# A list scheduler's ranking with slack, a shorter landing margin, and x rows loaded as nine and eight, in the training step of a speech RNN-T joint

## The chip, the cores and the metric

One core of one Trainium2 chip runs the whole program. The metric is device time in microseconds (us), the median of several runs of one execution each. The core has five engines that work side by side: PE (TensorE, matmuls), ACT (ScalarE), DVE (VectorE), POOL (GpSimd) and SP (SyncE, which here only issues DMAs). They are tied together by semaphores; each engine takes its own instructions strictly in the order in which the program lists them.

## The reference

Forward pass of a small convolutional front end and a joint network, and the gradients of all of its inputs:

```python
def _fwd_reference(x, w1, w2, g, w_f, w_g, w_o):
    B, T, D = x.shape                       # 2, 16000, 256
    h = sum over i of einsum("btc,cd->btd", xp[:, i:i+T], w1[i])     # K = 3 taps, zero padded
    h = gelu(h)[:, ::2]                     # 8000 positions
    f = sum over i of einsum("btc,cd->btd", hp[:, i:i+T1], w2[i])
    f = gelu(f)[:, ::2]                     # 4000 positions
    fe = einsum("btd,de->bte", f, w_f)
    ge = einsum("bud,de->bue", g, w_g)      # g: 2 x 8 x 256
    j = tanh(fe[:, :, None, :] + ge[:, None, :, :])
    return einsum("btud,dv->btuv", j, w_o)  # 2 x 4000 x 8 x 256

out, vjp = jax.vjp(_fwd_reference, x, w1, w2, g, w_f, w_g, w_o)
return (out, *vjp(grad_out))                # grad_out: 2 x 4000 x 8 x 256
```

Everything in HBM is bf16. The output `out` and the given `grad_out` are the large arrays (33 MB each); x and its gradient have 16 MB each.

## The kernel before

**Tiling.** The 4000 positions of `f` of each batch are cut into chunks: batch 0 has one of 256, seven of 512 and one of 160, batch 1 seven of 512, one of 256 and one of 160; 18 chunks in all. A chunk of W positions uses 4W rows of x. Chunks of 512 and 256 are called whole, those of 160 are not (160 is no multiple of 128).

**Stages of a chunk.**

- `load_xc` brings the rows of x in, transposed by the DMA (tile XC: channels on partitions).
- `stage_a` computes the first convolution for odd and even positions (XC times W1, tiles HT), the second (HT times W2, tile FT) and FE = FT times WF. `conv_gelu` follows each convolution's matmuls with ACT's square and gelu and with DVE's work on the gelu's derivative (tiles g_sq, g_s, which end as G1o, G1e and G2). `to_rows` then turns FE by PE transposes (L656, PSUM tile psb) into a row form, FER.
- `stage_j` works on four pairs of the eight u. For each pair ACT computes tanh(FE + ge) in column form (JT, L788); DVE adds FER and GEB (JR, L801) and ACT takes its tanh (JR, L808) in row form. PE multiplies JR by grad_out (GWO, the gradient of w_o, kept in PSUM for the whole program); PE multiplies the transposed grad_out (GOT) by the transposed w_o (GOT,WT matmuls); a square of JT (JSQ, on ACT L845 or on DVE L847) and DVE's NGZ (L855) turn this into the gradient before the tanh, which ZS and in the end NGFE collect over u (L863); PE computes the output (WO,JT matmuls), which is cast to OUT_SB (ACT L423 or DVE L428) and stored.
- `stage_de` runs one chunk behind `stage_j`: NGFE times WFT gives GF (L943), GF times W2T gives GH (L971, L981), GH times W1T gives GX, the gradient of x (cast on ACT L425 or DVE L430, then stored). The weight gradients are matmuls of row forms (`wgrad`), each added by DVE to an accumulator in fp32 (ACC, L912). The gradient of w1 needs GH in rows (GHR, a DMA transpose) and rows of x (X, loaded by `load_x9` for whole chunks, by `load_x5` for the others).
- After the last chunk, DVE writes seven weight gradients as `w_out` tiles, and `store` and `gg_out` write the last ones.

The matmuls are all recorded by the helper `mm` (L412), the DMAs by `dma` (L438, L440).

**Rows of x.** Partition p of a whole chunk with nb blocks (4 for 512 positions, 2 for 256) holds nb consecutive positions. The gradient of w1 needs 5 rows of x for each position, 4 rows from one position to the next, thus 4 nb + 1 rows for each partition. `load_x9` brings 9 of these rows (9 x 256 values) in one load; a chunk of 512 has two such loads (h = 0 and 1), in the two buffers of class "x5", the second starting 8 rows after the first. `xrow` picks the row for block bl and tap f from them. All matmul groups of `wgrad` for w1 read both buffers.

**The order of the work.** Nothing is issued where it is written. The class `Flow` records each operation (`op`) with its engine or engines, a cost in ns from the small functions `c_pe`, `c_act`, `c_dve`, the buffers it reads and writes, and a position. `issue` then plays the whole program in a model, `run`: each engine e has a time T[e], and at each step the model looks at every operation whose inputs have been issued, takes for it the start s (the modelled end of its inputs plus a wake-up time WAKE, or the time at which a buffer of its class comes free), and picks, for each engine, the operation with the smallest pair (max(s, t), key). Among the engines the smallest pair wins. So an operation that can start now beats one that is more urgent but ready 10 ns later; among those that can all start at once the key decides. After a pass `backward` replaces the keys by the latest start times that this schedule allows; there are three such passes, the best order is kept and emitted. An operation with two engines in `eng` (casts by `evac`, JSQ, some shift copies) goes to whichever engine wins it, so the order also decides the engine.

A DMA is done in the model at

```python
o.done = ring[e] + 2000.0 + o.margin     # L241
```

where `ring` adds up the transfers' modelled durations (a transposing DMA `bytes / 256 * 1.25` ns) and `margin` is MARGIN = 6500 (L49) unless the call names another (FIRST = 500 for the first loads and weights, 2000 for grad_out of the first chunk). The margin is thus a time that the model leaves between the modelled arrival of data and the use of it; it makes SP issue the load earlier against the work, or the user wait in the model.

Buffers of a class are reused in turn: "go" (rows of grad_out) has 4, "got" (its transpose) 3, "x5" 2, PSUM "ps" 7.

Of the kernel before, what the change touches and what calls it, by code (L numbers as in the profile page):

```python
# [13 lines left out]
ACT = mybir.ActivationFunctionType  # L14
# [6 lines left out]
LOADQ, STOREQ = "SP", "SP"  # L21
# [22 lines left out]
class Flow:  # L44
# [1 line left out]


    WAKE = {"PE": 45.0, "ACT": 25.0, "DVE": 25.0, "POOL": 280.0, "SP": 60.0}
    MARGIN = 6500.0  # L49
    TAIL = {"PE": 180.0, "ACT": 130.0, "DVE": 95.0, "POOL": 40.0, "SP": 0.0}  # L50

    def __init__(self, ctx, tc):
# [9 lines left out]
    def buf(self, cls, shape, dtype, name):  # L62
        b = Buf(cls, shape, dtype, name)
        s = self.seq[cls]
        b.seq, s[0] = s[0], s[0] + 1
        return b
# [89 lines left out]
    def run(self, emit):  # L156
        T = {e: 0.0 for e in self.WAKE}
        avail = {e: [] for e in T}
        ring = {"SP": 0.0, "POOL": 0.0, "ACT": 0.0}
        lanes = {True: [], False: []}  # L160
        left, prog = len(self.ops), -1e12
        slots = {k: [[p, 0.0, []] for p, _, _ in v] for k, v in self.slots.items()}
        seq = {k: [v[0], 0, v[2]] for k, v in self.seq.items()}
        users, use = {}, {}
        for o in self.ops:
            o.left = 0
            for b in o.bufs:
                users[b] = users.get(b, 0) + 1
        for o in self.ops:
            for d in o.succ:  # L170
                d.left += 1
        num = 0

        def put(o):
            o.ready = max((d.done for d in o.deps), default=0.0)
            for e in o.eng:
                avail[e].append(o)

        for o in self.ops:
            if o.left == 0:  # L180
                put(o)
        while left:
            best = None
            for e, lst in avail.items():
                t, wake, cand = T[e], self.WAKE[e], None
                for o in lst:
                    if o.nb is not None and prog < o.nb:
                        continue
                    s = o.ready + wake
                    if o.work:  # L190
                        ln = lanes[e == "POOL"]
                        if len(ln) >= 8:
                            s = max(s, ln[-8] + wake)
                    for b in o.new:
                        st = seq[b.cls]
                        if not st[2] and st[1] != b.seq:
                            s = None
                            break
                        f = min((x[1] for x in slots[b.cls] if x[1] is not None), default=None)
                        if f is None:  # L200
                            s = None
                            break
                        s = max(s, f + wake)
                    if s is None:
                        continue
                    k = (max(s, t), o.key, o, e)
                    if cand is None or k < cand:
                        cand = k
                if cand is not None and (best is None or cand[0] < best[0]):
                    best = cand  # L210
            if best is None:
                prog = min((o.nb for lst in avail.values() for o in lst if o.nb is not None and o.nb > prog), default=None)
                assert prog is not None, "no operation can start"
                continue
            s, _, o, e = best
            if o.lead:
                prog = max(prog, o.pos)
            for x in o.eng:
                avail[x].remove(o)
            o.slotdeps = []  # L220
            for b in o.new:
                free = [i for i, x in enumerate(slots[b.cls]) if x[1] is not None]
                i = min(free, key=lambda i: (slots[b.cls][i][1], i))
                b.slot, slots[b.cls][i][1] = i, None
                if not seq[b.cls][2]:
                    o.slotdeps += slots[b.cls][i][2]
                slots[b.cls][i][2] = []
                seq[b.cls][1] += 1
                if emit:
                    b.t = slots[b.cls][i][0].tile(b.shape, b.dtype, name=b.name, tag=b.cls)  # L230
            T[e] = s + o.cost[o.eng.index(e)]
            if o.work:
                a = max(ring[e], T[e] - 400.0)
                if e == "POOL":
                    ring[e] = a + o.work
                    for q in ("SP", "ACT"):
                        if ring[q] > a:
                            ring[q] += o.work
                else:
                    ring[e] = max(a, ring["POOL"]) + o.work  # L240
                o.done = ring[e] + 2000.0 + o.margin  # L241
                lanes[e == "POOL"].append(o.done - o.margin)
            else:
                o.done = T[e] + self.TAIL[e]
            o.at, o.seqn = (e, s, T[e]), num
            num += 1
            if emit:
                o.inst = o.fn(e)
                for h in o.hold:
                    self.tc.add_manual_dep(o.inst.ins, h.inst.ins.name, mybir.DependencyInfo(  # L250
                        mybir.DependencyClass.Sync, mybir.DependencyReason.DATA), reason="order of the first loads")
            left -= 1
            for b in o.bufs:
                if b.cls is not None:
                    slots[b.cls][b.slot][2].append(o)
                users[b] -= 1
                if users[b] == 0 and b.cls is not None:
                    slots[b.cls][b.slot][1] = o.done
            for d in o.succ:
                d.left -= 1  # L260
                if d.left == 0:
                    put(d)
        return T["PE"] if not emit else T
# [15 lines left out]
def kernel(  # L279
# [20 lines left out]
    B, T, D = x.shape  # L300
# [7 lines left out]
    P = 128  # L308
# [125 lines left out]
    def dma(q, out, in_, r, w, bytes_, new=(), transpose=False, at=None, after=(), cost=None, hold=(), nb=None, margin=None):  # L434
        def go(e):
            eng_ = nc.sync if e == "SP" else nc.gpsimd if e == "POOL" else nc.scalar
            if transpose:
                return eng_.dma_start_transpose(out=out(), in_=in_())  # L438
            else:
                return eng_.dma_start(out=out(), in_=in_())  # L440
        c = 1260.0 if transpose else 400.0 if q == "SP" else cost or (750.0 if q == "POOL" else 100.0)
        return op(q, c, go, r=r, w=w, new=new, at=at, after=after, hold=hold, nb=nb, margin=margin,
                  work=bytes_ / 256 * 1.25 if transpose else bytes_ / 300.0)
# [75 lines left out]

    def load_x9(b, c0, nb, h, at, hold=()):  # L520

        X9 = buf("x5", [P, 9, D], BF16, "X9")
        src, new, r0 = x[b, 0:1, :], [X9], 0
        if c0 == 0 and h == 0:
            op("POOL", 150.0, lambda e: nc.gpsimd.memset(X9[0:1, 0:3, :], 0.0), w=[(X9, "a")], new=new, at=at)
            dma(LOADQ, lambda: X9[0:1, 3:9, :], lambda: x[b, 0:6, :].rearrange("(o f) d -> o f d", o=1),
                r=[], w=[(X9, "b")], bytes_=3072, at=at, cost=550.0)
            new, r0 = [], 1
        for k, (lo, hi) in enumerate(row_parts(r0, P)):
            dma(LOADQ, lambda lo=lo, hi=hi: X9[:].rearrange("p f d -> p (f d)")[lo:hi],  # L530
                lambda lo=lo, hi=hi: bass.AP(tensor=src.tensor, offset=src.offset + (4 * (c0 + nb * lo) - 3 + 8 * h) * D,
                                             ap=[[4 * nb * D, hi - lo], [1, 9 * D]]),
                r=[], w=[(X9, ("m", k))], bytes_=(hi - lo) * 4608, new=new, at=at, hold=hold, cost=550.0)
            new = []
        return X9

# [379 lines left out]
    def stage_de(g_, t0, dt):  # L916
        b, ci, c0, W = chunks[g_]
# [100 lines left out]
        hold_ = S["go"] if g_ < 2 else ()  # L1018
        if wh:
            X5 = [load_x9(b, c0, nb_of[g_], h, t0 + dt * 0.2, hold_) for h in range(nb_of[g_] // 2)]  # L1020
            xrow = lambda m, bl, f, d2: X5[bl // 2][:m, bl % 2 * 4 + f, d2 * P:(d2 + 1) * P]
        else:
            X5 = [load_x5(b, c0 + bl * P, min(P, Ws - bl * P), t0 + dt * 0.2, hold_) for bl, m in sblk]
            xrow = lambda m, bl, f, d2: X5[bl][:m, f, d2 * P:(d2 + 1) * P]
# [76 lines left out]
    def gg_out():  # L1101
# [43 lines left out]
       r=[(warm, 0)], w=[(warm, 1)])  # L1145
# [117 lines left out]
```

## Time and profile before

| what | before |
|---|---|
| runs (us) | 808.18, 805.31, 805.61, 808.00, 805.19 |
| median (us) | 805.61 |
| the profiled execution (us) | 808.18 |
| its span, first to last instruction (us) | 806.4 |
| PE's last matmul ends (us) | 799.1 |
| bytes moved by DMA, mean rate | 184.81 MB, 229 GB/s |
| POOL busy | 85.7 us, 11% |
| ACT tanh JT (L788), of the span | 183.1 us, 288 instructions |
| DVE NGZ (L855) | 151.8 us, 252 instructions |
| ACT tanh JR (L808) | 136.4 us, 128 instructions |
| landing of GOT (72 transposing DMAs), median | 6.6 us |
| landing of X (28 loads of 576 KB), median | 6.4 us |

The span is 1.8 us shorter than the time of the execution it comes from, and that execution was the slowest of the five. Busy time of one engine is the union of its instructions; in rows of a group, "busy" is that too, and the mean is the duration of one instruction, which for pipelined instructions is longer than their distance. In a line of the chain of waits, such as "PE GWO L412 <- ACT JR L808", the first part waits and the second is what ended last before it; the three figures are the microseconds in all, the number of waits and the longest. The granted clock is that of PE, 1.00 being full speed.

The stretches of the profile that the prediction uses are the start (0 to 20 us, loads and the first convolutions; 20 to 120, the first chunks), the long middle (120 to 795) and the end.

### The profile page before, as it was taken

The page shows a single profiled execution, that of the slowest core. Times are in us where ns is not written, and L with a number is a line of the kernel's source. Part 1 is how long each engine was busy: PE and PEld are TensorE (multiplying, and loading weights), DVE is VectorE, ACT ScalarE, POOL GpSimd, SP SyncE. Part 2 cuts the span into 40 slices and gives each one's busy share as a digit, 9 for nine tenths or more (in the row PEclk, how much of TensorE's full clock was granted, in tenths as well). Part 3 has the DMA queues.
Part 4 walks back from the last instruction along what each step waited for, and adds up shares of the span by engine and source line. Part 5 has one row for each costly group of instructions (what it writes and reads, how often), then busy time and mean ns, then how long its engine had stood idle before and what let it go on. Part 6 is the DMA issues. An engine that isn't in the chain of part 4 may idle for free.

```text
span 806.4 us, 16830 instructions
## 1 busy us (share of the span) xinstructions
PE 775.8 (96%) x6083; PEld 575.0 (71%) x6124; DVE 761.2 (94%) x1743; ACT 705.8 (88%) x1138; POOL 85.7 (11%) x256
## 2 busy tenths in 40 slices
PE   7889999999999999999999999999999999999996
PEld 6556668676776867777777667676776867778885
DVE  4989999999999999998989999999999999999894
ACT  5989999988898999997889999988898989997482
POOL 1001010100102001011010100000101001010121
PEclk9989999999999999999999999999999999999999
DMA  8999999999999999999999999999999999997995
GB/s 192 199 234 215 224 210 241 240 230 286 208 253 231 249 248 197 246 224 232 212 232 180 264 249 237 240 237 284 206 265 226 246 249 228 258 222 226 191 215 140
DMA packets 403360, 184.81 MB, mean 229 GB/s; under 512 B 326310, under 2 KB 394956, under 8 KB 403276
## 3 DMA queue, kind: packets, MB, share of 16 engines
q1 hardware_dynamic: 400764, 182.53, 102.5%
q10 hardware_dynamic: 2384, 1.18, 0.6%
q8 instruction: 48, 0.79, 0.4%
q14 instruction: 36, 0.29, 0.1%
q0 software_dynamic: 128, 0.03, 0.0%
HBM read 52.48 MB, written 50.34 MB: 128 GB/s over the span
## 4 chain that ended last, share of the span: by engine, by line
PE 46%; DVE 31%; ACT 17%; DMA 3%; issue 3%; SPq 1%; DVEq 0%; ACTq 0%
PE ps L412 39%; PE GWO L412 6%; DVE NGZ L855 6%; DVE ZS L863 5%; ACT JT L788 4%; ACT JSQ L845 3%; DVE g_s L603 3%; DVE JR L801 3%; ACT g_sq L599 2%; DVE ACC L912 2%; ACT JR L808 2%; ACT HT L601 2%; ACT OUT_SB L423 2%; DVE g_sq L614 2%; DMA X<-in_x_dram 1%
## 5 line engine op out<-in xcount | busy, mean ns | idle before, releaser
L788 ACT ACTIVATE JT<-FE,GE 128x512 bf16<-128x512 bf16 (+2 forms) x288 | 183.1, 676 | 7.9 <-PE ps L412 6.9
L412 PE MATMUL ps<-GOT,WT 128*128 128x512 bf16 (+3 forms) x640 | 152.5, 333 | 1.5 <-DVE NGZ L855 0.3
L412 PE MATMUL ps<-WO,JT 128*128 128x256 bf16 x1024 | 151.7, 272 | 2.3 <-DVE GH L981 1.7
L855 DVE SCALAR_TENSOR_TENSOR NGZ<-JSQ,ps 128x512 f32<-128x512 bf16 (+2 forms) x252 | 151.8, 607 | 0.0
L808 ACT ACTIVATE JR<-JR 128x1024 bf16<-128x1024 bf16 x128 | 136.4, 1071 | 9.1 <-DVE JR L801 9.0
L845 ACT ACTIVATE JSQ<-JT 128x1024 bf16<-128x1024 bf16 (+2 forms) x128 | 126.1, 985 | 15.6 <-DVE NGZ L855 14.7
L412 PE MATMUL GWO<-GO_R,JR 128*128 128x256 bf16 x1024 | 133.2, 274 | 3.3 <-ACT JR L808 3.1
L412 PEld LDWEIGHTS <-JT 128*128 128x128 bf16 x1024 | 99.0, 98 | 48.9 <-issue 4.4
L863 DVE TENSOR_TENSOR ZS<-ZS,NGZ 128x512 f32<-128x512 f32 (+2 forms) x216 | 131.2, 612 | 0.0
L423 ACT CAST OUT_SB<-ps 128x512 bf16<-128x512 f32 x192 | 110.4, 596 | 22.9 <-PE ps L412 19.3
L412 PEld LDWEIGHTS <-JR 128*128 128x128 bf16 x1028 | 99.6, 98 | 26.2 <-ACT JR L808 5.8
L412 PEld LDWEIGHTS <-WT 128*128 128x128 bf16 x1000 | 88.5, 98 | 37.0 <-issue 2.8
L412 PEld LDWEIGHTS <-W 128*128 128x128 bf16 x720 | 66.9, 99 | 57.0 <-issue 3.6
L412 PE MATMUL ps<-WT,GH 128*128 128x256 bf16 x732 | 97.1, 273 | 0.9 <-DVE NGZ L855 0.8
L412 PE MATMUL ps<-XC,W 128*128 128x512 bf16 (+4 forms) x432 | 94.8, 349 | 3.1 <-DMA XC<-in_x_dram 2.3
L412 PE MATMUL ps<-GHR,X 128*128 128x256 bf16 x768 | 90.5, 273 | 0.0
L801 DVE TENSOR_TENSOR JR<-FER,GEB 128x1024 bf16<-128x1024 bf16 x128 | 87.1, 685 | 0.0
L412 PEld LDWEIGHTS <-X 128*128 128x128 bf16 x768 | 74.9, 98 | 9.7
L412 PEld LDWEIGHTS <-GH 128*128 128x128 bf16 x732 | 71.2, 98 | 12.5 <-issue 1.9
L603 DVE SCALAR_TENSOR_TENSOR g_s<-g_sq,ps 128x512 bf16<-128x512 bf16 (+2 forms) x108 | 65.8, 611 | 13.7 <-ACT HT L601 9.7
L912 DVE TENSOR_TENSOR ACC<-ACC,ps 128x512 f32<-128x512 f32 x96 | 64.8, 678 | 8.5 <-PE ps L412 8.2
L599 ACT ACTIVATE g_sq<-ps 128x512 bf16<-128x512 f32 (+2 forms) x108 | 58.5, 545 | 11.0 <-PE ps L412 10.3
(127 smaller groups left out, 994.6 us busy)
## 6 DMA issues: line engine op xcount, KB each, us to landing
GO_R<-in_grad_out_dram SPq DMA_DIRECT2D x56, 512.0 KB, 5.4
out_dram<-OUT_SB SPq DMA_DIRECT2D x56, 512.0 KB, 4.6
X<-in_x_dram SPq DMA_DIRECT2D x28, 576.0 KB, 6.4
out_dram<-GX_SB SPq DMA_DIRECT2D x28, 512.0 KB, 6.2
GO_R<-in_grad_out_dram SPq DMA_DIRECT2D x8, 256.0 KB, 4.4
out_dram<-OUT_SB SPq DMA_DIRECT2D x8, 256.0 KB, 3.7
GOT<-GO_R SPq DMA_TRANSPOSE x72, 6.6
out_dram<-w_out SPq DMA_DIRECT2D x9, 128.0 KB, 1.9
```

What stands on the lines that cost most here:

```text
L412: nc.tensor.matmul(ps_ap, lhsT=lhsT, rhs=rhs, start=start, stop=stop)
L423: nc.scalar.copy(out=dst(), in_=src())
L599: op("ACT", c_act(W, True), lambda e, mt=mt, ps=ps: nc.scalar.activation(out=sq[:, mt, :W], in_=ps[:, :W], func=ACT.Square, scale=GELU_SQR ...
L601: go = op("ACT", c_act(W, True), lambda e, mt=mt, ps=ps: nc.scalar.activation(out=h_ap(mt), in_=ps[:, :W], func=ACT.Gelu_apprx_tanh), r=[p ...
L603: op("DVE", c_dve(W), lambda e, mt=mt, ps=ps: nc.vector.scalar_tensor_tensor(out=s[:, mt, :W], in0=sq[:, mt, :W], scalar=1.0, in1=ps[:, :W ...
L788: op("ACT", c_act(W, ptr=True), lambda e, j=j, mt=mt: nc.scalar.activation(out=JT[:, j, mt, :W], in_=S["FE"][:, mt, :W], func=ACT.Tanh, bi ...
L801: op("DVE", c_dve(n * 2 * D, 0.5), lambda e, lo=lo, n=n, m=m, JR=JR: nc.vector.tensor_tensor(out=JR[:m, lo % 2:lo % 2 + n], in0=S["FER"][: ...
L808: op("ACT", c_act(n * 2 * D), lambda e, lo=lo, n=n, m=m, JR=JR: nc.scalar.activation(out=JR[:m, lo % 2:lo % 2 + n], in_=JR[:m, lo % 2:lo % ...
L845: nc.scalar.activation(out=JSQ[:, :, :W], in_=JT[:, j, :, :W], func=ACT.Square)
L855: op("DVE", c_dve(W) + 6, lambda e, d2=d2, ps=ps, u=u, zap=zap, JSQ=JSQ: nc.vector.scalar_tensor_tensor(out=zap(), in0=JSQ[:, d2, :W], sca ...
L863: op("DVE", c_dve(W), lambda e, d2=d2, dst=dst, NGZ=NGZ: nc.vector.tensor_tensor(out=dst[:, d2, :W], in0=ZS[:, d2, :W], in1=NGZ[:, :W], op ...
L912: op("DVE", c_dve(512), lambda e: nc.vector.tensor_tensor(out=acc_ap().rearrange("p k d -> p (k d)"), in0=acc_ap().rearrange("p k d -> p ( ...
```

## The change

Three things, all in how the same computation is ordered and loaded:

1. `SLACK`: the model ranks an operation by max(s + slack, t) in place of max(s, t), with a slack of 300 ns on PE, 200 on ACT and DVE, 0 on POOL and SP. An operation whose inputs have been there for at least the slack ranks at t with its key; one that only just became ready ranks as if it started up to 300 (200) ns later. The time at which it is then modelled to start is max(s, t) as before.
2. `MARGIN` goes from 6500 to 3500 ns.
3. `load_x9` loads nine rows for each partition with h = 0 and eight with h = 1, which starts 9 rows after the first; `xrow` takes rows 0 to 8 from the first buffer and 9 to 16 from the second. For chunks of 256 there is only h = 0, with nine rows as before.

```diff
     WAKE = {"PE": 45.0, "ACT": 25.0, "DVE": 25.0, "POOL": 280.0, "SP": 60.0}
-    MARGIN = 6500.0
+    SLACK = {"PE": 300, "ACT": 200, "DVE": 200, "POOL": 0.0, "SP": 0.0}
+    MARGIN = 3500.0
...
             for e, lst in avail.items():
-                t, wake, cand = T[e], self.WAKE[e], None
+                t, wake, cand, slack = T[e], self.WAKE[e], None, self.SLACK[e]
...
-                    k = (max(s, t), o.key, o, e)
+                    k = (max(s + slack, t), o.key, o, e, max(s, t))
...
-            s, _, o, e = best
+            _, _, o, e, s = best
...
     def load_x9(b, c0, nb, h, at, hold=()):
 
+        nr = 9 - h
         X9 = buf("x5", [P, 9, D], BF16, "X9")
...
-            dma(LOADQ, lambda lo=lo, hi=hi: X9[:].rearrange("p f d -> p (f d)")[lo:hi],
-                lambda lo=lo, hi=hi: bass.AP(tensor=src.tensor, offset=src.offset + (4 * (c0 + nb * lo) - 3 + 8 * h) * D,
-                                             ap=[[4 * nb * D, hi - lo], [1, 9 * D]]),
-                r=[], w=[(X9, ("m", k))], bytes_=(hi - lo) * 4608, new=new, at=at, hold=hold, cost=550.0)
+            dma(LOADQ, lambda lo=lo, hi=hi: X9[:, 0:nr].rearrange("p f d -> p (f d)")[lo:hi],
+                lambda lo=lo, hi=hi: bass.AP(tensor=src.tensor, offset=src.offset + (4 * (c0 + nb * lo) - 3 + 9 * h) * D,
+                                             ap=[[4 * nb * D, hi - lo], [1, nr * D]]),
+                r=[], w=[(X9, ("m", k))], bytes_=(hi - lo) * 512 * nr, new=new, at=at, hold=hold, cost=550.0)
...
-            xrow = lambda m, bl, f, d2: X5[bl // 2][:m, bl % 2 * 4 + f, d2 * P:(d2 + 1) * P]
+            xrow = lambda m, bl, f, d2: (X5[0][:m, 4 * bl + f, d2 * P:(d2 + 1) * P] if 4 * bl + f < 9 else
+                                         X5[1][:m, 4 * bl + f - 9, d2 * P:(d2 + 1) * P])
```

Which operations change places, and which change engines, follows from the model alone. Compared by tile and shape, PE issues the same set of matmuls and SP as many DMAs (452 instructions) as before; casts, squares and shift copies that may run on two engines are shared out anew, and the order differs from the first convolutions on.

## The prediction

> **What bounds the kernel now.** I read the page's busy shares first, then the stretches, then PE's waits, then single rows.
>
> ```profile
> PE 775.8 (96%) x6083; PEld 575.0 (71%) x6124; DVE 761.2 (94%) x1743; ACT 705.8 (88%) x1138; POOL 85.7 (11%) x256
> ...
> 20.00:120.00 100.00, 89.33 (x625) 59.47 (x627) 96.89 (x231) 96.82 (x158) 10.84 (x30) 0.97 1.06 216
> 120.00:450.00 330.00, 327.12 (x2585) 243.80 (x2602) 319.47 (x710) 298.32 (x472) 34.88 (x101) 1.00 1.04 233
> 450.00:500.00 50.00, 47.97 (x357) 34.24 (x358) 49.69 (x104) 49.74 (x76) 3.38 (x14) 1.00 1.06 248
> 500.00:780.00 280.00, 276.67 (x2204) 209.15 (x2218) 269.83 (x623) 241.86 (x399) 28.51 (x82) 1.00 1.06 236
> 780.00:795.00 15.00, 15.00 (x163) 12.76 (x161) 11.84 (x45) 8.48 (x18) 4.09 (x11) 1.00 0.73 161
> ...
> 40.00:60.00 20.00, 16.66 (x97) 10.03 (x98) 17.73 (x45) 17.75 (x28) 1.34 (x6) 0.83 1.00 238
> ```
>
> Columns of a stretch: its length, busy time of PE, weight loads, DVE, ACT and POOL, granted clock, DMA share, GB/s. PE idles 2.9 + 2.0 + 3.3 + 0 = 8.2 us between 120 and 795, but 10.7 us between 20 and 120, where DVE and ACT are full (60 to 120: no idle time on DVE, 0.3 us on ACT). So two regimes: the start is limited by DVE and ACT, the rest by PE. Is PE really full when it is busy? Rows with equal matmuls back to back say so:
>
> ```profile
> 301.15 1.04 PE L412 MATMUL GWO<-GO_R,JR 128*128 128x256 bf16 x8
> 302.02 1.46 PE L412 MATMUL ps<-HT,W 128*128 128x512 bf16 x6
> 46.60 1.94 ACT L788 ACTIVATE JT<-FE,GE 128x512 bf16<-128x512 bf16 x3
> 43.39 1.28 DVE L428 CAST FE<-ps 128x512 bf16<-128x512 f32 x2
> ```
>
> Eight matmuls of 256 columns in 1.04 us, one lasting 0.273, start (1.04 - 0.273) / 7 = 0.110 us apart; those of 512, (1.46 - 0.379) / 5 = 0.216. In the same way a 512-column ACT tanh costs 0.61 and a DVE cast 0.60, less than their durations (0.734, 0.680). The program has 6,124 matmuls: 4,316 x 0.110 + 1,120 x 0.216 + 112 x 0.163 + 388 x 0.056 + 188 short ones at about 0.05 gives 766 us. PE's floor is thus 766 of 806.4; the other 40 are 5.5 before the first convolution (8.1 less 2.6 of warm-up and transposes), 7.3 after the last matmul (799.1), and some 27 of waits and slow clock. Only those 27 and part of the ends can be won.
>
> ```profile
> PE GWO L412 <- ACT JR L808: 3.1, 4, 1.0
> PE psb L656 <- DVE FE L428: 2.3, 2, 2.0
> PE ps L412 <- DVE NGZ L855: 2.1, 3, 1.1
> ```
>
> These are PE's waits from 20 to 120: on ACT's tanh of JR, on the FE casts, on DVE's NGZ. From 120 to 795 the same kinds come to 5.5 (1.8 NGZ, 1.8 + 0.5 FE, 0.8 GH, 0.6 others).
>
> The Trainium skill ("Perfetto Trace Analysis", section "Identifying the Most-Contended Engine") holds matmul busy time a bad measure and would have PE judged by its weight loads; these are at 71%, which would make DVE at 94% the engine to relieve, and by it the sum below would be DVE's 5.3 us alone. Against it stands the 0.110 us spacing, by which PE is full after 120.
>
> **The change, part by part.**
>
> *What is issued.* PE's 6,124 matmuls are the same in another order. Operations free to run on either engine move: of the GX casts 22 go from DVE to ACT, of the whole JSQ squares 18 from ACT to DVE, 10 FE casts to ACT, 7 FER casts to DVE. DVE: -22 x 0.60 (GX) + 18 x 0.60 (JSQ) - 6 x 0.60 - 4 x 0.3 (FE) + 7 x 0.5 (FER), less 1.6 for three short squares, a WT cast and shifts = -5.3 us. ACT: +22 x 0.47 - 18 x 0.95 + 6 x 0.47 + 4 x 0.23 - 5 x 0.89 - 2 x 0.47 and +2 for small ones = -6. Both engines get lighter because a square costs 0.95 on ACT and 0.60 on DVE. After 120 this hides under PE.
>
> *Start.* I add up the work in issue order: ACT's up to a JR tanh against PE's up to the GWO group that needs it; the largest excess is what PE must lose, beside the offset with which ACT began and its own idle time. Before, the largest are +6.8 us (19th tanh: ACT 110.3, PE 103.5) and +7.6 (FT of the fourth chunk: 102.2 and 94.6). After: +7.9 (17th tanh) and +7.0, but 0.9 of it is a WT cast that now stands ahead of ACT's first square, in a 6.5 us wait: 7.0 and 6.1. Gain 0.6. For DVE, up to NGFE of the third chunk, +5.4 becomes +2.3 (largest now +3.5): 1.9, not on top of ACT's gain. A second part: in 40 to 60 DVE and ACT idle 2.3 us each, though they limit this stage, because PE stood still at the FE transposes (2.0 us; no PE work lies between the FE matmuls and these transposes) and then ran at clock 0.83. In the new order 1.5 us of convolution and GOT matmuls lies between. I take 1.4 of the 2.3. Sum -2.0; bounds -4.5 (all 2.3 back, and half of the waits above) and +2.5 (ACT's sum at the 16th tanh is 5.2 longer, against 1.7 for PE).
>
> *Middle.* DVE's sum is 2 to 5 us further ahead of PE at every NGFE, and the least PE work ahead of the FE transposes is 1.1 us instead of 0.0 to 0.9. The 5.5 us of waits should fall by somewhat under half: -2.5. Bounds -5.5 (all gone) and +5.5 (as many again elsewhere).
>
> *Tail.* Rows of the end, before:
>
> ```profile
> 786.24 0.55 DVE L863 TENSOR_TENSOR NGFE<-ZS,NGZ 128x160 bf16<-128x160 f32 x2
> ...
> 787.02 0.30 PE L412 MATMUL ps<-NGFE,WT 128*128 128x160 bf16 x2
> 787.16 1.04 PE L412 MATMUL ps<-GHR,X 128*128 128x256 bf16 x8
> 788.17 1.47 PE L412 MATMUL ps<-WO,JT 128*128 128x256 bf16 x12
> ```
>
> The last chunk's chain NGFE, GF, GH runs from PE to DVE and back; 24 GHR,X and 16 WO,JT matmuls (40 x 0.110 = 4.4 us) fill its waits. In the new order all 40 stand ahead of the last GOT matmuls. After the last GHR,X, DVE still does one ACC add (0.66), three NGZ, one ZS and two NGFE (1.5): 2.2 us; then NGFE,WT 0.35, GF with the reduction ahead of it 1.0, both GF groups with the GFS copy 1.1, the last GH 0.4: 5.0 us, in which PE has 2.7 of its own. PE stands 2.3 us; bounds 0 and 4.4. Against it: SP's OUT_SB stores and one w_out, which from 794.40 kept the GX stores waiting until 796.77, now stand ahead of the GHR transpose; the last GX cast ends at 795.42, so the seven w_out stores can start 1.35 us earlier (bounds -1.4 and 0). Sum +1.0.
>
> For this wait the skill has a rule that speaks against the change: "TensorE: Matmul & The Clock Gate", section "HAM oscillation — how this bites in real kernels", lets PE idle no longer than about 3.4 us before its clock is halved. Here 40 to 45, with PE busy 1.76 of 5 us, was followed by a granted 0.55 in 45 to 50. The 2.3 us stay below the rule; at 4.4, some 60 matmuls behind it would take 0.213 instead of 0.110 and add 6 us to the sum.
>
> *Landing margin 3500 for 6500.* By line 241 and what surrounds it the model now lets a GOT transpose land 8.9 us after its issue (0.86 + 2.56 + 2 + 3.5) instead of 11.9. The trace has 4.7 / 6.6 / 9.1 (least, median, most), and PE waits 0.2 us for GOT in all. SP's lead barely moves: GOT stands 2 or 3 stores ahead of OUT_SB as before, never less than 1 after the first. Cost 0; bounds 0 and +3 (72 transposes, one in twelve late by half a microsecond).
>
> *x rows, 9 and 8.* Fourteen loads move 128 x 512 bytes less: 0.92 of 184.8 MB, 4 us of DMA time at 229 GB/s. PE never waits for X, so nothing is won; each gradient matmul group already waited for both buffers, so nothing is added. SP's instructions stay 452.
>
> **Sum.** -2.0 - 2.5 + 1.0 = -3.5 us against the span of 806.4, which gives 802.9. The profiled execution took 808.18, 1.8 outside its span and 2.6 above the median of 805.61; I take the difference over to the median: 802.1.
>
> **Rivals.** (1) *The tail decides, slower.* All 4.4 us of cover are exposed, and SP's earlier stores win nothing because DVE's last adds wait for PE. With nothing won at the start or in the middle: 810.0. It decides from where those two return less than 2. For it: the order is certain. Against: PE has matmuls of its own in the chain. 0.16. (2) *Waits only move*: PE is full after 120, and the start is set by ACT, whose envelope gains only 0.6; the two traces differ in place, not in sum: 805.0. For it: ACT's longer sums early on. 0.20. (3) *The margin bites*: GOT lands late, PE waits at pair starts: +3 and up, 808.6. Against: 0.2 us now. 0.06; ACT's longer sum at the start, 0.04 more. (4) *More is won*: all bounds to the good side at the start and half in the middle, -8: 797.6. 0.12. That the order hardly changes is excluded: it differs from the first convolutions on.
>
> **Numbers.** Forecast 0.42 (798.5 to 803.2), with (4) 0.54 for faster by over 0.3% (below 803.2; 0.3% is about what a measurement of this kernel tells from no change), 0.20 within, 0.26 slower (above 808.0). Range 796.8 to 809.8: under 0.1 below it and about 0.1 above.
>
> **What would show it.** Right: PE idle from 20 to 120 down from 10.7 to 8 or 9, the 2.0 us wait on FE gone and the clock in 40 to 60 above 0.83; waits from 120 to 795 near 3; about 2 us of idle PE between the last GOT and the last GX matmuls; DVE near 756, ACT near 700. Wrong: PE waits for DMA of over 1 us (margin), ACT with more than 6 us of idle time from 20 to 120, or a tail clock well below 1.

## The result, and the profile after

| | runs | median (us) | lowest to highest |
|---|---|---|---|
| before, as known when predicting | 5 | 805.61 | 805.19 to 808.18 |
| before, all runs | 80 | 807.52 | 804.42 to 812.20 |
| changed | 43 | 804.51 | 800.16 to 809.59 |

Taken side by side the ratio is 0.9967, with a 95% interval of 0.9957 to 0.9977: the change wins 2.7 us, 0.33%. The forecast was a gain of 3.5 us (0.44%). The time itself, 802.1, came out 2.4 us too low, and most of that is the start it was counted from: the five runs of before had a median 1.9 us below that of eighty.

The profiled execution of the changed kernel took 807.67 us (span 805.9), 3.2 us above its kernel's median. So the two traces differ by only 0.5 us; they show well what was exchanged for what, and badly how much was won in all. The granted clock changes from run to run too: its mean over the 43 runs lies between 0.987 and 0.999, so a slow stretch of the clock in this one trace need not be in the others. The busy shares of the changed kernel's page:

```profile
PE 776.1 (96%) x6082; PEld 575.2 (71%) x6124; DVE 758.2 (94%) x1729; ACT 701.2 (87%) x1150; POOL 91.4 (11%) x258
```

PE has as much to do as before, DVE and ACT a little less. The changed kernel's stretches (columns as before):

```profile
20.00:120.00 100.00, 88.72 (x623) 58.77 (x627) 96.22 (x230) 97.48 (x161) 10.18 (x30) 0.99 1.10 223
120.00:450.00 330.00, 328.34 (x2599) 245.31 (x2616) 322.40 (x710) 295.50 (x476) 38.02 (x104) 1.00 1.06 233
450.00:500.00 50.00, 46.99 (x354) 33.62 (x355) 48.42 (x103) 47.36 (x73) 5.80 (x12) 1.00 1.08 227
500.00:780.00 280.00, 276.62 (x2214) 210.33 (x2227) 268.66 (x617) 243.08 (x409) 30.10 (x87) 0.99 1.07 234
780.00:795.00 15.00, 13.40 (x118) 9.86 (x116) 10.28 (x37) 4.76 (x11) 3.38 (x9) 0.83 0.78 169
...
40.00:60.00 20.00, 18.96 (x137) 12.21 (x136) 20.00 (x53) 19.84 (x32) 1.47 (x6) 1.00 1.12 235
```

The stretch from 40 to 60 is repaired: PE busy 18.96 us for 16.66, clock 1.00 for 0.83, DVE and ACT full. Yet from 20 to 120 PE idles 11.3 us, more than the 10.7 of before, and from 120 to 780 it idles 8.05 for 8.24. The waits say why. PE's waits from 20 to 795 us in the changed kernel:

```profile
PE ps L413 <- DMA GFR<-GF: 4.2, 2, 2.8
PE GWO L413 <- ACT JR L810: 3.3, 5, 1.0
PE ps L413 <- ACT JT L790: 1.9, 4, 1.1
PE ps L413 <- DVE G1o L623: 1.3, 1, 1.3
PE ps L413 <- DVE NGFE L865: 1.2, 2, 0.8
PE ps L413 <- DVE g_s L605: 1.0, 2, 0.6
PE ps L413 <- DMA GOT<-GO_R: 1.0, 1, 1.0
```

From 20 to 780, the waits on NGZ (3.8 us before) are gone, those on FE went from 4.5 to 0.4, those on GH from 1.9 to 0. In their place stand waits for DMAs: 6.3 us for 0.2, most of them for GFR, NFR and GHR, the transposes that bring computed tiles into row form for the weight gradients; and some on other results of DVE and ACT (JT 1.9, G1o 1.3, g_s 1.0, ACC and ACCF 1.6). All waits of this stretch together: 15.4 us before, 16.7 after.

Why GFR was late shows in SP's queue. In the changed kernel DVE finished GF at 98.4 us:

```profile
98.41 0.60 SPq L441 DMA_DIRECT2D out_dram<-OUT_SB  x1
99.11 1.84 SPq L439 DMA_TRANSPOSE NFR<-NGFE  x1
101.06 4.96 SPq L439 DMA_TRANSPOSE XC<-in_x_dram  x2
106.12 2.95 SPq L439 DMA_TRANSPOSE GOT<-GO_R  x1
109.17 0.55 SPq L441 DMA_DIRECT2D GO_R<-in_grad_out_dram  x1
109.77 1.34 SPq L439 DMA_TRANSPOSE GFR<-GF  x1
```

Second column: how long the instruction held SP. GFR was issued 11.4 us after its data were there, behind two XC transposes, a GOT and a GO_R. In the kernel before, GF was done at 101.2 us and GFR stood ahead of the XC transposes:

```profile
102.97 2.40 SPq L438 DMA_TRANSPOSE GFR<-GF  x1
105.48 7.12 SPq L438 DMA_TRANSPOSE XC<-in_x_dram  x2
```

The model books 1.26 us of SP for any transpose; in the changed kernel GOT held SP for 3.7 us in the median (1.24 to 6.25). By these bookings and a margin of 3.5 us, GFR was in time for PE even at the end of this queue. On the chip PE arrived first and waited 2.8 us, and after that the clock was 0.75 in the mean from 116 to 119 and 0.68 from 119 to 122, against 1.00 from 110 to 113.

### The profile page after: what moved, and what is told of

The parts are those of the page before. It is cut to its first block, busy times and chain, and to the rows that moved or that the text cites. A ratio compares the mean times of both kernels' runs of the same rounds, so it can differ in the third digit from the quotient of the medians.

```text
span 805.9 us, 16819 instructions
## 1 busy us (share of the span) xinstructions
PE 776.1 (96%) x6082; PEld 575.2 (71%) x6124; DVE 758.2 (94%) x1729; ACT 701.2 (87%) x1150; POOL 91.4 (11%) x258
## 4 chain that ended last, share of the span: by engine, by line
PE 61%; DVE 26%; DMA 6%; ACT 4%; issue 2%; SPq 1%; DVEq 0%; ACTq 0%
PE ps L413 51%; PE GWO L413 9%; DVE NGZ L857 4%; DVE ZS L865 3%; DVE g_s L605 3%; DMA GFR<-GF 2%; DMA GOT<-GO_R 2%; DVE JR L803 2%; DVE g_sq L616 1%; DVE GH L973 1%; DVE OUT_SB L429 1%; DVE GH L983 1%; DMA W<-in_w_dram 1%; DVE GF L945 1%; DVE ZS L857 1%
## 5 line engine op out<-in xcount | busy, mean ns | idle before, releaser
L790 ACT ACTIVATE JT<-FE,GE 128x512 bf16<-128x512 bf16 (+2 forms) x288 | 187.0, 689 | 0.1
L424 ACT CAST OUT_SB<-ps 128x512 bf16<-128x512 f32 x193 | 115.5, 603 | 24.4 <-PE ps L413 24.1
L847 ACT ACTIVATE JSQ<-JT 128x1024 bf16<-128x1024 bf16 (+2 forms) x113 | 109.8, 972 | 13.2 <-DVE NGZ L857 12.2
L413 PE MATMUL ps<-XC,W 128*128 128x512 bf16 (+4 forms) x432 | 92.6, 342 | 2.5 <-DMA XC<-in_x_dram 1.8
L601 ACT ACTIVATE g_sq<-ps 128x512 bf16<-128x512 f32 (+2 forms) x108 | 59.9, 555 | 14.1 <-PE ps L413 9.1
```

Of the source, the lines that this page charges most:

```text
L413: nc.tensor.matmul(ps_ap, lhsT=lhsT, rhs=rhs, start=start, stop=stop)
L424: nc.scalar.copy(out=dst(), in_=src())
L601: op("ACT", c_act(W, True), lambda e, mt=mt, ps=ps: nc.scalar.activation(out=sq[:, mt, :W], in_=ps[:, :W], func=ACT.Square, scale=GELU_SQR ...
L790: op("ACT", c_act(W, ptr=True), lambda e, j=j, mt=mt: nc.scalar.activation(out=JT[:, j, mt, :W], in_=S["FE"][:, mt, :W], func=ACT.Tanh, bi ...
L847: nc.scalar.activation(out=JSQ[:, :, :W], in_=JT[:, j, :, :W], func=ACT.Square)
```

## The experiments

All comparisons are with runs of before on the same chip. `issue` makes four orders: one by the written positions, and one after each of three backward passes; it emits the one with the shortest end by the model. Before took the first backward order; the changed kernel took the order by positions. That turned out to matter, so most later runs fix it with `issue(passes=0)`. "Waits" are PE's from 20 to 780 us in the run's trace, all of them, and of these those for DMAs and for FE.

| run | slack PE / ACT, DVE | margin, row transposes / rest | order | median | ratio (95%) | waits: all, DMA, FE |
|---|---|---|---|---|---|---|
| rows_same_order | 0 | 6500 | backward | 806.74 | 0.9992 (0.9978 to 1.0005) | 16.2, 1.1, 4.8 |
| rows_only | 0 | 6500 | backward | 804.18 | 0.9980 (0.9967 to 0.9993) | 16.1, 1.3, 4.9 |
| before_pass0 | 0 | 6500 | positions | 806.23 | 1.0002 (0.9990 to 1.0014) | 14.1, 0.0, 5.8 |
| margin_only | 0 | 3500 | positions | 806.83 | 0.9998 (0.9983 to 1.0013) | 16.6, 2.0, 4.9 |
| noslack_margin_rows | 0 | 6500 / 3500 | positions | 802.79 | 0.9950 (0.9936 to 0.9964) | 16.8, 0.0, 4.0 |
| changed kernel | 300 / 200 | 3500 | positions | 804.51 | 0.9967 (0.9957 to 0.9977) | 16.7, 6.3, 0.4 |
| after_310_210 | 310 / 210 | 3500 | positions | 803.29 | 0.9950 (0.9930 to 0.9969) | 15.2, 6.2, 0.4 |
| after_290_190 | 290 / 190 | 3500 | positions | 799.99 | 0.9907 (0.9884 to 0.9931) | 11.0, 3.2, 1.1 |
| margin_rows_3500 | 300 / 200 | 3500 / 6500 | positions | 804.13 | 0.9970 (0.9956 to 0.9983) | 14.3, 4.2, 0.2 |
| slack_only | 300 / 200 | 6500 | positions | 802.24 | 0.9944 (0.9927 to 0.9961) | 9.9, 1.3, 0.0 |
| slack_rows_pass0 | 300 / 200 | 6500 | positions | 800.57 | 0.9927 (0.9911 to 0.9944) | 9.5, 0.0, 0.0 |
| slack_290_190 | 290 / 190 | 6500 | positions | 800.34 | 0.9922 (0.9903 to 0.9940) | 11.9, 1.1, 1.1 |
| margin_9500 | 300 / 200 | 9500 | positions | 801.76 | 0.9941 (0.9925 to 0.9957) | 10.9, 0.4, 0.0 |
| slack_pe | 300 / 0 | 6500 | positions | 799.16 | 0.9912 (0.9897 to 0.9926) | 11.1, 0.5, 0.8 |
| slack_adve | 0 / 200 | 6500 | positions | 798.40 | 0.9888 (0.9865 to 0.9911) | 10.3, 2.3, 1.6 |
| margin_rows_6500 | 300 / 200 | 6500 / 3500 | positions | 797.02 | 0.9885 (0.9869 to 0.9901) | 11.2, 0.4, 1.8 |
| pe_margin_rows | 300 / 0 | 6500 / 3500 | positions | 796.31 | 0.9856 (0.9835 to 0.9878) | 12.1, 1.4, 1.0 |
| slack_310_210 | 310 / 210 | 6500 | backward | 804.72 | 0.9976 (0.9962 to 0.9989) | 13.3, 0.0, 1.7 |
| slack_rows | 300 / 200 | 6500 | backward | 810.16 | 1.0045 (1.0029 to 1.0061) | 17.7, 0.0, 2.1 |

The x rows are nine and eight in all of them but margin_only, before_pass0, slack_only, slack_290_190 and slack_310_210.

**One part alone, and the changed kernel with the old margin.** SLACK, MARGIN and the x rows each by itself, then slack and x rows together:

```diff
-    MARGIN = 6500.0
+    SLACK = {"PE": 300, "ACT": 200, "DVE": 200, "POOL": 0.0, "SP": 0.0}    # slack_only, slack_rows
+    MARGIN = 3500.0                                                        # margin_only
+        nr = 9 - h                                                         # rows_only, slack_rows
```

> Only SLACK; margin 6500 and the x rows as before. Theory A (slack wins at the start, the short margin gives part of it back through late row transposes): PE's waits for DMA between 20 and 795 us stay near the 0.2 us of before (6.4 us in the changed kernel), the wait on FE is gone as in the changed kernel, and the time is 2 to 6 us below the changed kernel's 804.5, about 801. Theory B (every new order is a draw, whatever its rule): 803 to 809 with waits of other kinds in place of those gone. Theory C (the margin wins, slack does nothing): the time of before, 807.5.

> Only MARGIN 3500; no slack, the x rows as before. Theory A: PE waits 3 to 7 us more for DMA (GFR, GHR, NFR, GOT) than before, the wait on FE stays, time 2 to 5 us above before, 810 to 812. Theory B: within 3 us of before either way. Theory C: the whole gain, 804.5.

> Only the x rows in nine and eight; no slack, margin 6500. The order changes from the middle on, since the model books 64 KB less for 14 loads. Theory A and C: no change, within 1 us of before (807.5), 0.92 MB less moved, no PE wait for X. Theory B: up to 2 us either way although nothing is gained or lost by the loads themselves.

> The changed kernel with MARGIN back at 6500 (slack and x rows stay). Theory A: the 6.4 us that PE waits for DMA in the changed kernel shrink to under 1 us, and the time falls to 800 to 802.5. Theory B: 802 to 808. Theory C: back to about 807.5.

Slack alone won 0.56%, at least as much as the whole change (their intervals overlap a little); the margin alone showed no gain or loss; and slack with the x rows lost 0.45%, which none of my theories had. The sum of the parts is not the whole, since each part makes a new order of everything. But slack_rows differed from slack_only in one more thing: its order was that of the second backward pass.

**Which keys.**

```diff
-    F.issue()
+    F.issue(passes=0)
...
-    SLACK = {"PE": 300, "ACT": 200, "DVE": 200, "POOL": 0.0, "SP": 0.0}
+    SLACK = {"PE": 290, "ACT": 190, "DVE": 190, "POOL": 0.0, "SP": 0.0}
```

> slack_rows (810.2) with issue(passes=0): the order by the written positions is emitted, as in slack_only (802.2) and in the changed kernel, in place of that of the second backward pass, which the model had put 1.1 us shorter. Theory P (with slack, the position keys make good orders on the chip and the backward keys bad ones, whatever the model's end says): 801 to 804. Theory L (every order is a draw): anywhere from 801 to 811. Theory R (the rows of nine and eight are what costs under slack): 807 or more.

> The kernel before with issue(passes=0): no slack, margin 6500, x rows as before, but the order by positions; the order of before came from the first backward pass. Theory P in its strong form (the keys alone are the gain, slack is nothing): about 802 to 803. Theory P with slack as a needed part: 805 to 808. Theory L: 801 to 811.

> slack_only with a slack of 290 and 190 ns for 300 and 200, a change without a meaning of its own; the model again keeps the order by positions. Theory P, and the theory that slack itself helps (S): 801 to 804. Theory L: 801 to 811, and a distance of over 3 us from slack_only would be the size of the draw.

> slack_only with a slack of 310 and 210 ns; here the model keeps the order of the second backward pass, 2.6 us shorter by its own account. Theory P: 806 to 811. Theory S: 801 to 804. Theory L: 801 to 811.

slack_rows by positions: 800.57 in place of 810.16, from the keys alone. Positions without slack: nothing (1.0002). A slack of 290 instead of 300: the same gain. A slack of 310, with the backward order that the model then preferred: 0.24% won, 804.7, which lies between what theories P and S gave. So here slack with the position keys wins 0.6 to 0.8%, the position keys alone win nothing, and slack with backward keys won 0.24% once and lost 0.45% once; theory R (the rows cost) fell. PE's waits from 20 to 795 us, before_pass0:

```profile
PE ps L413 <- DVE NGZ L857: 3.3, 5, 1.4
PE psb L658 <- DVE FE L429: 3.0, 5, 1.7
PE psb L658 <- ACT FE L424: 2.8, 9, 0.5
PE GWO L413 <- ACT JR L810: 2.7, 2, 2.1
```

and slack_rows_pass0:

```profile
PE GWO L413 <- ACT JR L810: 7.2, 6, 3.7
PE ps L413 <- DVE NGFE L865: 1.7, 1, 1.7
PE ps L413 <- DVE ACC L914: 1.1, 3, 0.5
...
PE ps L413 <- DVE NGZ L857: 0.3, 1, 0.3
```

The waits on NGZ and FE (9.1 us, then 0.3) are what slack removes here; a wait on ACT's tanh at the start, where ACT is the limit, grows by 4.5.

**The margin.** slack_rows_pass0 differs from the changed kernel only in MARGIN. Its SP queue at the same place:

```profile
100.67 2.65 SPq L439 DMA_TRANSPOSE NFR<-NGFE  x1
103.41 1.26 SPq L439 DMA_TRANSPOSE GFR<-GF  x1
104.78 6.31 SPq L439 DMA_TRANSPOSE XC<-in_x_dram  x2
```

GFR goes out 2.3 us after GF, ahead of the XC transposes; PE uses it 8.5 us after the issue (6.8 in the changed kernel) and does not wait. The next runs gave the longer margin to the row transposes alone, or to all else alone, or lengthened it:

```diff
         dma("SP", ..., w=[R],
-            bytes_=KT * n * P * P * 2, new=[R], transpose=True, nb=nb, at=at)
+            bytes_=KT * n * P * P * 2, new=[R], transpose=True, nb=nb, at=at, margin=6500.0)
...
+    MARGIN = 3500.0      # margin_rows_6500; the same for HR, HRs and GHR
+    MARGIN = 6500.0      # margin_rows_3500, with margin=3500.0 in the calls; slack_pe
+    MARGIN = 9500.0      # margin_9500
```

> The changed kernel (slack, margin 3500, x rows; order by positions) with 6500 for the DMA transposes of computed tiles alone (HR, FR, NFR, GFR, GHR). Theory A (the short margin costs where PE waits for these transposes: 5.4 of the 6.4 us of DMA waits in the changed kernel): PE's DMA waits from 20 to 795 us fall to about 1, and the time to 801 to 802. Theory L (the 4 us between margins 3500 and 6500 are a draw of the order): 800 to 806 without relation to the DMA waits.

> The counterpart: 6500 everywhere, 3500 for HR, FR, NFR, GFR and GHR alone; slack, x rows, order by positions. Theory A: DMA waits on GFR, NFR or GHR of 3 to 6 us and 803 to 805. Theory L: 800 to 806.

> Slack, x rows, order by positions, margin 9500 everywhere (800.6 with 6500, 804.5 with 3500). Theory A: PE waits for no DMA at 6500 any more, so nothing is won: 800 to 802, and a longer margin may push work apart for nothing. A linear effect of the margin: 797.

> Slack on PE alone (300), 0 on ACT and DVE; margin 6500, x rows, order by positions (806.2 without any slack, 800.6 with all). Theory F (slack works because PE no longer takes a group whose inputs became ready at that moment by the model, such as the FE transposes, and so tolerates a late cast): PE's waits on FE under 1.5 us and 800 to 802. If the slack of ACT and DVE is what works: 805 to 807, waits on FE of 4 to 6 us as without slack.

margin_rows_6500 beat its expectation by 4 us (797.02), its counterpart fell where the changed kernel lies, and lengthening further won nothing. DMA waits are 0.4 us in the first, 4.2 in the second:

```profile
PE GWO L413 <- ACT JR L810: 3.5, 6, 1.1
PE ps L413 <- DVE NGFE L865: 2.5, 2, 1.8
PE psb L658 <- DVE FE L429: 1.8, 2, 1.5
PE ps L413 <- ACT JT L790: 1.7, 3, 1.1
```

are the largest waits of margin_rows_6500 (20 to 795 us), and in margin_rows_3500 the second largest is

```profile
PE ps L413 <- DMA NFR<-NGFE: 2.9, 2, 2.5
```

The DMA waits don't explain all of it: margin_rows_6500 is also 3.5 us faster than slack_rows_pass0, which has none. There the granted clock differs. From 20 to 120 us, slack_rows_pass0 and then margin_rows_6500:

```profile
20.00:120.00 100.00, 91.53 (x638) 61.52 (x641) 97.49 (x235) 96.62 (x159) 10.37 (x29) 0.97 1.03 217
20.00:120.00 100.00, 91.63 (x659) 61.62 (x663) 98.72 (x235) 99.86 (x166) 9.32 (x30) 1.00 1.06 220
```

At the end slack_rows_pass0 ran at 0.50 from 783.5 to 790.2, margin_rows_6500 at 1.00. Over their runs the mean clock is 0.992 (0.989 to 0.994) and 0.997 (0.995 to 1.000) in the median; 0.005 of some 775 us of PE work is an estimate of 3.9 us, about the whole distance.

**What the rest tells apart.** The slack of the other engines, both finds together, the x rows with every engine's order as before (the model books the old size), and the changed kernel with a meaningless change of slack:

```diff
+    SLACK = {"PE": 0.0, "ACT": 200, "DVE": 200, "POOL": 0.0, "SP": 0.0}     # slack_adve
+    SLACK = {"PE": 300, "ACT": 0.0, "DVE": 0.0, "POOL": 0.0, "SP": 0.0}     # pe_margin_rows
-                r=[], w=[(X9, ("m", k))], bytes_=(hi - lo) * 512 * nr, ...
+                r=[], w=[(X9, ("m", k))], bytes_=(hi - lo) * 4608, ...        # rows_same_order
```

> Slack on ACT and DVE alone (200), 0 on PE; margin 6500, x rows, order by positions (806.2 with no slack, 799.2 with PE's slack alone, 800.6 with all three). Theory F (PE's slack is the part that works): 804.5 to 807, PE waiting 4 to 6 us on FE as without slack. If either slack does it: 799 to 802.

> Both finds together: slack on PE alone, margin 6500 for the transposes of computed tiles and 3500 for the other loads, x rows, order by positions (797.0 with the same margins and all slacks, 799.2 with PE's slack alone and 6500 everywhere). If the two gains add as 0.3 % and 0.4 %: 795.5 to 796.5. If what is left is a draw: 796 to 801.

> The kernel before with the loads of nine and eight rows, while the model still books 4608 bytes for each partition, so that every engine's order is that of before; only the 14 shorter loads differ. My prediction: no change, 806.2 within 1 us. If the 0.92 MB less of traffic help (as rows_only's 804.2 might say): 804 to 805.

> The changed kernel (margin 3500, x rows, order by positions) with a slack of 290 and 190 for 300 and 200: a change without meaning, which shows how much of its 804.5 is a draw. Theory A (the short margin is bad for the row transposes in any such order): 802.5 to 806 and DMA waits of 3 to 7 us. Theory L: 797 to 806.

Theory F fell: slack on ACT and DVE alone does as much as slack on PE alone. The x rows in themselves are nothing (0.9992, its interval holds 1), so what rows_only won (0.2%, its interval overlaps this one) is put down to its order. And after_290_190 came out 4.5 us faster than the changed kernel by a slack 10 ns smaller, though GFR still was late (2.1 us):

```profile
PE GWO L413 <- ACT JR L810: 4.4, 8, 1.1
PE ps L413 <- DMA GFR<-GF: 2.1, 1, 2.1
PE ps L413 <- ACT JT L790: 1.7, 3, 1.1
```

So a single pair of orders can't price the margin. Two last runs:

> The best margins (6500 for the transposes of computed tiles, 3500 for the rest), x rows, order by positions, but no slack on any engine (797.0 with slack 300 and 200, 796.3 with PE's alone). If slack is the gain and the margins only keep it: 804 to 808, with PE's waits on FE of 4 to 6 us. If these margins are good in themselves: 797 to 801.

> The changed kernel with a slack of 310 and 210 (order by positions): a third draw at margin 3500 beside 804.5 (300, 200) and 800.0 (290, 190). If the changed kernel is the unlucky draw: 798 to 802. If 290 was the lucky one: 803 to 806. In both PE waits 3 to 7 us for DMA, as far as the short margin is what makes those waits.

after_310_210 (an order that keeps the changed kernel's PE sequence for its first 2,420 matmuls and weight loads of 12,248, so no independent draw) again has 6.2 us of DMA waits and 0.9950. Without slack the best margins give 0.9950, between the two expectations; slack on top of them gives 0.9885 and 0.9856. Yet noslack_margin_rows has no fewer waits than before (16.8 for 15.4): its trace differs in the clock from 20 to 120 (1.00 for 0.97) and at the end.

Over all orders by positions with slack: the eight with 6500 or more for the row transposes have ratios of 0.9909 in the mean, the four with 3500 there 0.9949. The difference of 0.4%, 3.2 us, goes with DMA waits of 0.9 and 5.0 us in the mean; its standard error by the spread of the single orders (0.3%) is 0.18%. But three of the eight have slack on some engines only, and these are among the fastest; the five with slack on all three engines have 0.9924, which leaves 0.25% (2.0 us, standard error 0.2%). Single pairs differ: against the changed kernel, slack_rows_pass0 (another margin alone) is 0.4% faster and margin_rows_6500 0.8%; but with a slack of 290 (slack_290_190 and after_290_190, which differ in the x rows too) and without slack (before_pass0 and margin_only) the short margin cost nothing. So the DMA waits come with the short margin; that they cost time is likely, not certain.

Slack is surer: the twelve with it have 0.9922 in the mean, the three without it 0.9983, and in the three pairs that differ in slack alone (0.9944 against 1.0002; 0.9885 and 0.9856 against 0.9950, one partner for both) it wins 0.58 to 0.94%, that is 4.7 to 7.6 us. With margin 3500 throughout, the changed kernel against margin_only, it is 0.3%. PE's idle time from 120 to 780 us says the same with less scatter: 6.8 to 8.6 us in the three without slack, 3.2 to 5.7 in the eight with slack and the long margin for the row transposes, 2.0 to 8.1 in the four with the short one.

The best version, pe_margin_rows, takes 0.9856 of before (0.9835 to 0.9878), 796.31 us, less than either kernel. Its busy shares:

```profile
PE 773.3 (97%) x6124; PEld 573.2 (72%) x6124; DVE 743.2 (94%) x1709; ACT 722.0 (91%) x1182; POOL 78.8 (10%) x246
```

## Why the prediction was right and wrong

**Direction right, the size near, by terms that were not.** Predicted -2.0 (start) - 2.5 (middle) + 1.0 (tail) + 0 (margin) + 0 (x rows) = -3.5; measured -2.7. That the two are near is luck: slack won more than I had for it, and the margin, which I had at nothing, took part of it back. In the changed kernel's own trace it is the rival "waits only move" that fits (15.4 us of waits before, 16.7 after), and two of the signs that I had named for being wrong are there: DMA waits of over 1 us (6.3) and a tail clock well below 1 (0.50).

**The margin: the step that failed.** "The model now lets a GOT transpose land 8.9 us after its issue ... Cost 0". I priced the margin by GOT alone, which has stores and loads enough around it. The same constant governs GFR, NFR and GHR, which become ready late in a chunk and stand behind other transposes in SP's queue; SP's lead was counted for GOT and not for them. In the trace of before PE used GFR 5.7 to 13.0 us after its issue, the last chunk aside; in the changed kernel it is 4.7 to 12.0, with landings of up to 6.7. The cost is 6.1 us more of DMA waits in the changed kernel, and, likely, 2.0 to 3.2 us of time by the means over orders, near the upper bound (+3) of this term, which the rival "the margin bites" starts from; that rival had GOT as the late one, which accounts for only 1.0 of the 6.3 us. The order of SP was there to be read before: GFR behind XC and GOT.

**Start and middle: right in what goes, too small without the short margin, too large with it.** FE's 2.0 us wait and the clock of 0.83 are gone, as forecast. I took somewhat under half of the middle's 5.5 us of waits on NGZ, FE and GH; all of them went. Where the margin takes nothing back, slack is worth the 4.7 to 7.6 us above, not 4.5. In the changed kernel's own trace the start gained nothing (idle 11.3 instead of the forecast 8 to 9), because GFR, GHR and NFR took 3.9 us there. Nor did its middle: the waits from 120 to 795 are 7.4 us, where I had forecast about 3 and before had 5.5; 2.5 of them are for DMAs, 2.9 for G1o, ACC and ACCF, 1.2 for NGFE at the tail. slack_rows_pass0, with the long margin, has 3.8.

**The tail: sum right, by luck.** I had 2.3 us of standing PE, 4.4 as a bound, and -1.35 for the earlier stores, and took the clock as safe. PE stood for less, two waits of 1.2 us in all on NGFE, but in this execution half the clock followed them. From the stretches of the changed kernel:

```profile
786.00:788.00 2.00, 2.00 (x25) 1.50 (x22) 1.63 (x6) 0.00 (x0) 0.82 (x1) 1.00 1.01 307
788.00:790.00 2.00, 0.74 (x6) 0.37 (x6) 1.93 (x12) 0.00 (x0) 0.88 (x4) 0.98 0.82 186
790.00:792.00 2.00, 2.00 (x16) 1.54 (x14) 1.19 (x6) 0.62 (x2) 0.84 (x3) 0.50 0.41 110
792.00:794.00 2.00, 1.79 (x12) 1.04 (x11) 0.71 (x3) 0.60 (x1) 0.30 (x2) 0.50 0.34 66
794.00:796.00 2.00, 2.00 (x11) 1.40 (x10) 0.00 (x0) 0.60 (x1) 0.00 (x0) 0.50 0.91 191
```

PE idles 1.3 us in 788 to 790 and then works six microseconds and more at half speed, which loses about 2.9 us from 790 to 796 (5.79 busy at 0.50): some 4.4 us with the idle time behind it. PE ends at 802.1 instead of 799.15. On the other side the span ends 3.8 us after that (7.3 before): SP issues the seven w_out stores from 799.16 on (799.52 before), though PE ends 3 us later. Net about +1; predicted +1.0. The clock that makes up this sum was 1.00 after the same two waits in after_310_210.

**x rows: right**, 0 by rows_same_order. **Engine shares: right in sign**, DVE 761.2 to 758.2 (forecast 756), ACT 705.8 to 701.2 (700).

**The baseline.** The difference was carried to a median of five runs that lay 1.9 us under the kernel's long-run median; a range for the time has to hold that too.

**What stays open.** Why the backward keys spoil what slack wins was not taken apart, nor why one order keeps the full clock from 20 to 120 and at the end and another doesn't; nor was any version with the last chunk's order mended. Either engine's slack does the work alone, and I have no run that says through which operations.

## What to carry to other kernels

A planner that ranks work by the moment it becomes ready builds a schedule in which every estimate must be exact; letting just-ready work rank a few hundred nanoseconds later removed most waits on fresh results and, with the order by positions, won 0.6 to 0.9% where the row transposes kept their margin. A safety margin for transfers has to be judged by the transfer with the longest queue ahead of it, not by the most frequent one: here late row transposes took 3 to 6 us of PE's time as waits and likely a good part of the gain, and the long margin for them alone removed these waits. And where any edit reshuffles the whole order, one kernel is one draw (here a standard deviation of 0.3%): try neighbours that differ in nothing of meaning before giving a gain to its cause. The model's own end ranked nothing: over 20 orders its correlation with the measured ratio is -0.06 (783.6 us for margin_only, 802.1 for margin_9500), that of PE's waits 0.74.

## What the runs showed of the hardware that I had not expected

The clock fell after less idle time than I had taken as safe. The Trainium skill ("TensorE: Matmul & The Clock Gate", section "HAM oscillation — how this bites in real kernels") speaks of gaps over about 3.4 us. In the changed kernel two gaps of 0.84 and 0.35 us within 1.5 us, with short matmuls between, were followed by 0.50 from 790 to 796. In after_310_210, the same two waits and another of 0.8 us left the clock at 1.00 throughout. In these traces a gap's price is therefore not set by its length alone: the 2.8 us on GFR were followed by 0.50 from 117.5 to 120.8, waits of 1.3 and 0.7 us on G1o and ACCF by 0.50 from 520.3 to 523.6, and the two short gaps at the end by 0.50 from 790.0 to 796.7, twice as long.

In the changed kernel's trace a transposing DMA held the queue that issues it: GOT 1.2 to 6.3 us on SP (3.7 in the median), GHR 4.1 and XC 2.6 in the median, where a plain load or store held it for about 0.6. What sets the spread of GOT no run here shows.
